# Fourier mixing with a soft mixture of experts, one core: two copies, one product and one pair of products moved in the written order

## The chip, the cores and the metric

The kernel runs on 1 core of one Trainium2 chip. The metric is the device time in microseconds of one execution. Engines are named as in the profile: PE (TensorE, matmuls; PEld its weight loads), DVE (VectorE), ACT (ScalarE), POOL (GpSimd) and SP (SyncE, whose queue issues most of the DMAs).

## The reference

```
X  = rfft(x, axis=1)                       # x: 8 batches, 2496 positions, 256 channels
Yr = Xr @ w_r - Xi @ w_i + b_r;  Yi = Xr @ w_i + Xi @ w_r + b_i
Y  = soft threshold of Yr and of Yi at 0.01
y  = irfft(Y)                              # the tokens, 8 * 2496 of them
logits = y @ phi                           # 32 slots = 8 experts x 4
d = softmax of logits over all tokens;  slot_input = d.T @ y
slot_out[e] = relu(slot_input[e] @ w1[e]) @ w2[e]
out = (softmax of logits over the slots) @ slot_out
```

All is float32. The softmax over tokens runs over all batches, so a running maximum and running sums go from batch to batch; the expert layers and the output come after the last batch.

## The kernel before, in words

The transform of length 2496 is split into 39 times 64. The work of one batch goes through stages, and at any moment three batches are in the kernel, each in another stage.

*First transform (`a_group`, L475 to L504).* From batch 2 on, a batch has 22 columns in six groups q: five of four columns and a last half group of two. POOL makes sums and differences of input rows (xh, xl), PE forms two products pa into two PSUM buffers, the first always in a buffer with the tag pf, the second with the tag that `PLAN["aqt"]` names: for the fifth group (q = 4) that is ps, for the half group pt. ACT copies the two products to the tile ast, at the times `PLAN["aqo"]` behind the group's own time: 0.4 and 0.7. A full ast tile is stored to DRAM by SP (`a_store`).

*Second transform and linear layer (`f2`, `lin_k`, `lin_y`, `tp_p`).* A batch has five steps s of four units of time each, so a batch has 20 units. In each step the stored data (ap) comes back, PE forms px twice, ACT and DVE split it into high and low parts (xsm and xth by ACT, then xsm and xtl by DVE, then xsh by ACT and xsl by POOL), PE forms pk and two products py, DVE adds them to ut, and the threshold gives rt. `tp_p` then multiplies with phi (pq), ACT copies the result to lg, and PE transposes it.

*Slot stage (`c_stages`, L795).* It runs for batches 0 to 6 beside later batches' transforms, with its time counted from t0 = 20 b + 26. `halves` (L752) does each of its four matrix products in two halves: for each half ACT makes a high part (the tiles chpg, chpL, chpe, chpd), DVE or POOL a low part (clpg and so on), and later PE does three matmuls into a PSUM buffer and an engine evacuates it. The four are pg (to g_sb, then through DRAM as gd and gp), pL (to L, the logits), pe (to ea, then through DRAM as ed and eb) and pd (to dd). Between pL and pe lie the maximum over tokens (DVE's mx, PE's pm, DVE's mall and dg, PE's pb) and the exponential ee. `running` (L899) forms the factor fo of the running maximum: two operations on DVE, then an exp on ACT at 12.2 + 0.4 units. pg and pe use the tag ps, which has a single buffer; so do pm and pb; pL uses ps and pt.

*Order.* No engine chooses: every engine and SP's queue run their instructions in program order. Program order comes from a heap of generators, each of which yields the time at which its next piece is written (`step_to`, `run_until`). The times stand in `PLAN`, some with other values for the last batches under `"late"`. They are units of that order only, and about 2.5 us of the trace go to one unit in the middle of the kernel.

```
"pL": [7.05, 8.02],          # the two halves' matmuls, behind t0
"pe": [12.02, 12.98],
"cl": [0.9, 0.4, 0.3],       # high part 0.9 ahead of the first matmul, second half 0.4 later, low part 0.3 later
```

In `halves` the evacuation of a half is written 0.25 behind its matmuls. `f2` writes the second px of a step at 4 (s - 1) + 2 units and its first two copies 0.59 later; `lin_y` writes the first half of a step's second py at 4 s + 2.35.

*After the last batch* the expert weights (loaded beforehand) are used in `mlp1` and `mlp2`, and the output is formed in blocks (pq, ost) and written by 41 DMAs.

Of the kernel before, what the change touches and what calls it, by code (L numbers as in the profile page):

```python
# [79 lines left out]
def _constants():  # L80
# [83 lines left out]

PLAN = {
    "aq": [-9.55, -5.55, -1.55, 2.45, 6.45, 7.4],
    "aqo": [0.4, 0.7],
    "aqt": ["pt", "pt", "pr", "pr", "ps", "pt"],
    "eo": {0: [5.0, 3.0], 4: [5.0, 4.95], 5: [2.05, 2.0]},
    "xq": [8.55] * 5 + [7.5],  # L170
    "aq2": {(2, 0): [6.6, 8.8, 9.2, 10.45], (2, 1): [8.8, 11.2, 11.6, 14.45]},
    "th": 'PA',
    "sh": 'A',
# [3 lines left out]
    "pL": [7.05, 8.02],  # L177
    "pm": 9.05,
    "pb": 10.32,
    "pe": [12.02, 12.98],  # L180
    "cm": 14.3,
    "pd": [19.05, 20.02],
    "pr": [20.48, 20.49, 24.48, 24.49, 28.49],
# [7 lines left out]
    "ko": 0.915,  # L191
    "to": 0.4,
    "ws": [-29, -28.9, -28.8, 2],
    "late": {'6': {'cms': [13.1, 13.2, 18, 22.65, 22.66, 22.67], 'pd': [16.681, 16.6], 'pdt': ('pl', 'pl'), 'pda': 1, 'pLt': ('ps', 'ps'), 'pr': [17.15, 18.3, 20.179, 19.707, 19.902], 'pL': [6.6, 7.3], 'pm': 8.51, 'pmr': 9.35, 'pb': 10.36, 'pe': [11.747, 11.96, 12.419], 'pg': [0.875, 1.275], 'fr': {'sinv': 0, 'm2': 0, 'f1': 0, 'suni': 0}, 'pbx': 1.2, 'pet': ('pf', 'pf'), 'so': 0.2}, '5': {'so': 1.5}, '4': {}},
    "T_": {'wl': [[-31, 't', 1], [-30, 't', 1], [-29, 't', 1], [-21.8, 't', 1], [-20.6, 't', 1], [-16.9, 't', 2], [-16.8, 't', 2], [-16.6, 't', 2], [-16.1, 't', 2], [-15.6, 't', 2], [-14.8, 'z', 2], [-14.6, 'z', 2], [-14.1, 'z', 2], [-13.6, 'Y', 1], [-13.1, 'Y', 1], [-12.4, 'c', 2], [-11.8, 's', 1], [-11.2, 'a', 1], [-10.6, 'a', 1], [-10, 'a', 1], [-9.5, 'Ww_r', 1], [-8.7, 'Wnws', 1], [-8.6, 'Wwd', 1], [0.01, 'k', 1], [0.01, 'u', 1], [0.02, 'x', 2], [0.02, 'x', 2], [0.02, 'x', 2], [1.4, 'R', 2], [1.4, 'R', 2], [1.73, 'Z', 2], [1.74, 'Z', 2]], 'cl': 2.0, 'cp': 46.5, 'ct': 46.6, 'du': [[2.55, 2]], 'd1': [], 'cm': [19.9, 19.91, 19.92, 25, 25.1, 25.2], 'cm7': [0.71, 1.7, 1.95, 2.7, 2.71, 2.8], 'ye': 0.2, 'te': [[5.6, 0.2], [5.5, 0.4]], 'pg': [-15.49, -11.49, -7.99, -3.934, -2.9], 'yt': 0.578, 'wr': -30.6, 'tp': [0, 0.6, 0.85, 0.5], 'tt': [0.4, 0.55, 0.821, 1.25, 0.994], 'z': 1.686, 'th': [0.1, 0.12], 'tl': [0.24, 0.25], 'pgt': ['ps', 'ps', 'ps', 'pf', 'pf'], 'ch': [0.263, 0.5, 0.7, 1.0, 1.514, 2.0], 'te7': 'AAAAAAAAAA', 'op': 2, 'ot': [3, 5, 7], 'gt': [-14.5, -10.5, -7.0, -3.93, -2.89]},
    "f1": [-1.6, -1.5],
    "kw": [[-28.6, 4], [-28.4, 12]],
# [62 lines left out]
def fourier_soft_moe_kernel(ctx: ExitStack, tc: tile.TileContext, t: dict, out: bass.AP):  # L260
# [18 lines left out]
    def psum(tag, name):  # L279
        return pp.tile([128, 512], F32, tag=tag, name=name, bufs=psum_bufs[tag])  # L280

    def wtile(shape, dt, tag, name):
        if tag in a_bufs:
            return wap.tile(list(shape), dt, tag=tag, name=name, bufs=a_bufs[tag])
        if tag in main_bufs:
            return wmp.tile(list(shape), dt, tag=tag, name=name, bufs=main_bufs[tag])
        return wcp.tile(list(shape), dt, tag=tag, name=name, bufs=chain_bufs[tag])
# [44 lines left out]
    def mm(**kw):  # L332
        tc.keep_in_program_order(nc.tensor.matmul(**kw))  # L333
# [11 lines left out]
    def load_x(i, q=sp):  # L345
        if i >= len(xorder) or xorder[i] in xrs:
            return
        b, g = xorder[i]
        ng = min(xc, G - g)
        xr = wtile([PX, xc, D], F32, "xr", f"xr{b}_{g}")  # L350
        q(out=xr[:, :ng, :], in_=x[b, :, g : g + ng, :])
        xrs[(b, g)] = xr
# [45 lines left out]
    ident, sgn, suni, sinv, dsc, dmask = (cols[k] for k in ("ident", "sgn", "suni", "sinv", "dsc", "dmask"))  # L398
    f1, m2 = cols["f1"][:P1], cols["m2"][:Q1]
# [75 lines left out]
    def a_group(b, q):  # L475
        n = GP if q < 5 else 1
        tx, te, to, tu = PLAN["aq2"].get((b, q), [20 * (b - 1) + PLAN["aq"][q] - d for d in (PLAN["xq"][q], *PLAN["eo"].get(q, PLAN["eo"][0]), 0)])
        yield tx
        load_x(xorder.index((b, 4 * q)))
        if q == 0:  # L480
            ad[b] = dr.tile([128 + 1, G, D], F32, tag="adr", name=f"adr{b}", bufs=3)
        xv = xrs[(b, 4 * q)].rearrange("p (g a) d -> p g a d", a=2)[:, :n]
        eo = []
        for i, z in enumerate(("xh", "xl")):
            yield (te, to)[i]
            eo.append(wtile([128, GP, D], F32, z, f"{z}{b}_{q}")[:, :n])
            P.tensor_tensor(out=eo[i], in0=xv[:, :, 0], in1=xv[:, :, 1], op=(ALU.add, ALU.subtract)[i])
        yield tu
        po = [psum(("pf", PLAN["aqt"][q])[i], f"pa{b}_{q}_{i}") for i in range(2)]
        for i in range(2):  # L490
            for c in range(2):
                rows = slice(64 * i, 64 * i + 64)
                mm(out=po[i][64 * c : 64 * c + 64, : n * D], lhsT=f1t[rows, 64 * c : 64 * c + 64], rhs=eo[c][rows],
                   start=True, stop=True, skip_group_check=True)
        for i in range(2):
            yield tu + PLAN["aqo"][i]
            g = 4 * q + n * i
            gs = next(a for a in abounds_[2] if a[0] <= g < a[1])
            if g == gs[0]:
                asts[(b, g)] = wtile([QA, 6, D], F32, "ast", f"ast{b}_{g}")  # L500
            ast = asts[(b, gs[0])]
            A.copy(out=ast[:, g - gs[0] : g - gs[0] + n, :].rearrange("p g d -> p (g d)"), in_=po[i][:, : n * D])
            if g + n == gs[1]:
                step_to(a_store(tu + PLAN["aqo"][i] + (1.35 if q == 5 else 0.75), b, ast, gs))  # L504

    def a_store(t0, b, ast, gs):
        yield t0
        a_write(ad[b], ast, *gs)
# [4 lines left out]
    def a_write(adr, ast, g0, g1, r0=0, r1=QA, q=sp):  # L513
        q(out=adr[r0:r1, g0:g1], in_=ast[r0:r1, : g1 - g0, :])
# [236 lines left out]

    def halves(n, t0, times, out, const, fr, src, evac, tags=("ps", "ps"), ev=0.25):  # L752
        xs = []
        for h in range(2 * fr[n]):
            yield t0 + (PLAN["chp"][h] if n == "suni" else times[0] - PLAN["cl"][0] + PLAN["cl"][1] * h)
            x = src(h)
            m, w = x.shape[0], x.shape[1] * x.shape[2]
            xh, xl = (
                wtile([128, 352], F32R, z, f"{z}{out[0]}_{h}")[:m, :w].rearrange("p (k s) -> p k s", s=S)
                for z in ("ch", "cl")  # L760
            )
            A.copy(out=xh, in_=x)
            yield t0 + (PLAN["clp"][h] if n == "suni" else times[0] - PLAN["cl"][0] + PLAN["cl"][1] * h + PLAN["cl"][2])
            {"V": V, "P": P}[PLAN["cl_"][n][h]].tensor_tensor(out=xl, in0=x, in1=xh.bitcast(F32), op=ALU.subtract)
            xs.append((xh, xl))
        for h in range(2):
            yield t0 + times[h]
            ps = psum(tags[h], f"{out[0]}_{h}")
            if fr[n]:
                ch, cl = const_hl[n]  # L770
                for i, (w_, x_) in enumerate(((ch, xs[h][0]), (cl, xs[h][0]), (ch, xs[h][1]))):
                    mm(out=out[1](ps), lhsT=w_, rhs=x_, start=i == 0, stop=i == 2)
            else:
                mm(out=out[1](ps), lhsT=const, rhs=src(h), start=True, stop=True)
            yield t0 + times[h] + ev
            evac(h, out[1](ps))
# [18 lines left out]
    def c_stages(b):  # L795
# [5 lines left out]
        g_sb = wtile([128, K1, S], F32, "g_sb", f"g_sb{b}")  # L801
        fr = K_["fr"]
        yield from halves(
            "sinv", t0, K_["pg"], (f"pg{b}", lambda ps: ps[:, :320]), sinv, fr,
            lambda h: p_sb[:, h * 10 : h * 10 + 10, :],
# [9 lines left out]
        yield t0 + K_["pL"][0] - PLAN["cl"][0] - 0.01  # L815
        gp_wrap(gp)
        yield from halves(
            "m2", t0, K_["pL"], (f"pL{b}", lambda ps: ps[:, :352]), m2, fr,
            lambda h: gp[:, h * 11 : h * 11 + 11, :],
# [167 lines left out]
    def step_to(gen):  # L987
        t = next(gen, None)
        if t is not None:
            heapq.heappush(heap, (t, next(seq), gen))  # L990
# [200 lines left out]
    for b in range(2, B):  # L1191
        for q in range(6):
            step_to(a_group(b, q))
# [231 lines left out]
    so = [wtile([128, D], F32R, "gp", f"so{i}") for i in range(2)]  # L1425
# [101 lines left out]
```

## Time and profile before

| | |
|---|---|
| median of 3 runs (504.04 to 506.6) | 504.19 us |
| the profiled execution | 506.02 us |
| its span, first to last instruction | 504.2 us |
| mean granted TensorE clock | 0.984 |
| PE busy | 479.7 us, 95% |
| DVE busy | 360.4 us, 71% |
| ACT busy | 315.9 us, 63% |
| POOL busy | 266.3 us, 53% |

A busy share says which engine is short of time, not what one place costs. For that one looks at the places where PE's row of matmuls has a hole, and at what the profile names as the releaser. In a timeline a line has the start, the duration, the engine, the operation and, in brackets, the idle time in front of it with the releaser; matmuls overlap, so their durations are longer than the distances between their starts.

### The profile page before, as it was taken

How to read it: one execution, taken by the hardware profiler on the slowest of the kernel's cores; microseconds unless marked ns; L12 is line 12 of the kernel's file. 1: busy time of each engine (PE TensorE's matmuls, PEld its weight loads, DVE VectorE, ACT ScalarE, POOL GpSimd, SP SyncE). 2: the span in 40 equal slices, each digit the busy share in tenths (PEclk: the TensorE clock that was granted, in tenths of full speed). 3: DMA queues.
4: the chain of work that ended last, by engine and by line, in shares of the span. 5: the costliest groups of instructions: out<-in, count | busy, mean ns of one | idle time of the engine just before them, and what ended most of it. 6: DMA issues, size and time to landing. Idle time of an engine off the chain costs nothing.

```text
span 504.2 us, 11938 instructions
## 1 busy us (share of the span) xinstructions
PE 479.7 (95%) x4438; PEld 392.4 (78%) x4438; DVE 360.4 (71%) x718; ACT 315.9 (63%) x724; POOL 266.3 (53%) x277
## 2 busy tenths in 40 slices
PE   8879999999999999999999999999999999999990
PEld 5479879788878877888788888879898777468880
DVE  3245996787878877987698769877976585446771
ACT  4357557667757775677577767775656556147770
POOL 0035777766956695769666966682344412322210
PEclk9988999999999999999999999999999999999996
DMA  8988698477969596959596969584878799449998
GB/s 294 319 288 303 237 281 257 140 249 231 289 185 301 156 299 200 296 151 326 144 309 161 320 189 318 112 307 119 240 174 246 294 400 387 171 162 401 404 405 332
DMA packets 90461, 131.04 MB, mean 260 GB/s; under 512 B 40204, under 2 KB 61836, under 8 KB 90404
## 3 DMA queue, kind: packets, MB, share of 16 engines
q1 hardware_dynamic: 89460, 128.16, 77.8%
q10 hardware_dynamic: 944, 2.13, 1.2%
q8 instruction: 35, 0.57, 0.5%
q14 instruction: 22, 0.18, 0.1%
HBM read 69.25 MB, written 50.00 MB: 237 GB/s over the span
## 4 chain that ended last, share of the span: by engine, by line
PE 70%; DVE 10%; DMA 10%; ACT 5%; issue 2%; SPq 1%; POOL 1%; ACTq 0%; DVEq 0%; POOLq 0%
PE py L333 16%; PE pq L333 10%; PE px L333 10%; PE pa L333 9%; PE pk L333 7%; PE pt L708 3%; PE pr L333 2%; DMA gd<-g_sb 2%; DMA gp<-gd 2%; PE pc L708 2%; PE pg L333 2%; DMA xr<-in_x 2%; DVE ut L256 2%; PE pe L333 1%; PE hps L333 1%
## 5 line engine op out<-in xcount | busy, mean ns | idle before, releaser
L256 POOL TENSOR_TENSOR xsl<-xsm,xsh 128x256 fp32r<-128x256 f32 x77 | 64.8, 843 | 112.1 <-ACT xsh L256 108.5
L256 DVE SCALAR_TENSOR_TENSOR ut<-py,pk,k 128x256 f32<-128x256 f32 x160 | 69.7, 477 | 29.0 <-PE py L333 27.7
L333 PE MATMUL px<-smov,ap 128*128 128x128 f32 x640 | 85.1, 277 | 1.3 <-ACT ast L256 1.3
L333 PEld LDWEIGHTS px<-smov,ap 128*128 128x128 f32 x640 | 79.5, 194 | 2.5 <-ACT ast L256 1.7
L256 ACT COPY ast<-pa 128x512 f32<-128x512 f32 (+1 forms) x88 | 48.1, 556 | 23.2 <-PE pa L333 23.1
L256 DVE TENSOR_TENSOR xtl<-px,xth 128x512 fp32r<-128x512 f32 x80 | 54.3, 680 | 0.1
L256 ACT CAST xth<-px 128x512 fp32r<-128x512 f32 x80 | 47.4, 594 | 6.8 <-PE py L333 5.9
L333 PE MATMUL py<-xth,nwsh 128*128 128x256 f32 (+1 forms) x160 | 51.4, 321 | 0.0
L256 DVE TENSOR_TENSOR xsm<-px,xsm 128x256 f32<-128x256 f32 x80 | 33.1, 414 | 25.5 <-ACT xth L256 14.0
L256 POOL TENSOR_TENSOR rt<-ut,rt 128x512 f32<-128x512 f32 x36 | 50.2, 1395 | 0.1
L333 PE MATMUL pk<-xsh,w_rh 128*128 128x256 f32 (+1 forms) x160 | 47.8, 299 | 0.0
L256 ACT COPY xsm<-px 128x256 f32<-128x256 f32 x80 | 29.9, 373 | 28.3 <-PE px L333 27.5
L256 POOL TENSOR_TENSOR xh<-xr 128x512 f32<-128x512 f32 (+1 forms) x36 | 44.7, 1241 | 1.0 <-DMA xr<-in_x 0.9
L333 PE MATMUL pk<-xsl,w_rh 128*128 128x256 f32 (+1 forms) x160 | 44.9, 281 | 0.3 <-POOL xsl L256 0.3
L333 PE MATMUL py<-xth,wdh 128*128 128x256 f32 (+1 forms) x160 | 45.1, 282 | 0.0
L333 PE MATMUL py<-xtl,nwsh 128*128 128x256 f32 (+1 forms) x160 | 44.9, 280 | 0.0
L333 PE MATMUL py<-xth,nwsl 128*128 128x256 f32 (+1 forms) x160 | 44.8, 280 | 0.0
L333 PE MATMUL py<-xtl,wdh 128*128 128x256 f32 (+1 forms) x160 | 44.8, 280 | 0.0
L333 PE MATMUL pk<-xsh,w_rl 128*128 128x256 f32 (+1 forms) x160 | 44.7, 279 | 0.0
L333 PE MATMUL py<-xth,wdl 128*128 128x256 f32 (+1 forms) x160 | 44.7, 279 | 0.0
L256 POOL TENSOR_TENSOR xl<-xr 128x512 f32<-128x512 f32 (+1 forms) x36 | 43.3, 1204 | 0.0
L256 ACT CAST xsh<-xsm 128x256 fp32r<-128x256 f32 x80 | 33.0, 412 | 16.4 <-DVE xsm L256 16.4
(227 smaller groups left out, 1274.7 us busy)
## 6 DMA issues: line engine op xcount, KB each, us to landing
ap<-adr SPq DMA_DIRECT2D x76, 256.0 KB
out<-ost SPq DMA_DIRECT2D x37, 512.0 KB
xr<-in_x SPq DMA_DIRECT2D x35, 512.0 KB
adr<-ast SPq DMA_DIRECT2D x20, 768.0 KB
y<-z SPq DMA_DIRECT2D x112, 96.0 KB
w<-in_moe_w SPq DMA_DIRECT2D x21, 512.0 KB
adr<-ast SPq DMA_DIRECT2D x7, 512.0 KB
w<-in_moe_w SPq DMA_DIRECT2D x14, 256.0 KB
```

The lines of the kernel that those rows point to most:

```text
L256: return lambda *a, **k: self.tc.keep_in_program_order(f(*a, **k))
L333: tc.keep_in_program_order(nc.tensor.matmul(**kw))
L708: tc.keep_in_program_order(nc.tensor.transpose(out=out, in_=in_, identity=identity))
```

## The change

Three edits of the written order; no instruction is added or taken away.

1. The second ast copy of the fifth and of the half group of `a_group` is written 0.5 behind the group's time in place of 0.7 (the third entry of `aqo`, picked by `2 * i`). For the fifth group this is between lg (at 0.45 on this scale) and xsh. The store of the half group's tile hangs on the same time and moves by 0.2 as well.
2. The first half of pe is written at 12.36 in place of 12.02, behind the first half of the second py (12.35). Its high and low parts keep their times: `first` in `halves` takes 12.02 for f1 from the new entry `clb`. The evacuation moves along, from 12.27 to 12.61.
3. In batch 5 the second half of pL is written at 7.95 in place of 8.02, so ahead of the px at 8.0.

```diff
-    "aqo": [0.4, 0.7],
+    "aqo": [0.4, 0.7, 0.5],
...
-    "pe": [12.02, 12.98],
+    "pe": [12.36, 12.98],
+    "clb": {"f1": 12.02},
...
-    "late": {... '5': {'so': 1.5}, '4': {}},
+    "late": {... '5': {'so': 1.5, 'pL': [7.05, 7.95]}, '4': {}},
...
         for i in range(2):
-            yield tu + PLAN["aqo"][i]
+            yield tu + PLAN["aqo"][i if q < 4 else 2 * i]
...
             if g + n == gs[1]:
-                step_to(a_store(tu + PLAN["aqo"][i] + (1.35 if q == 5 else 0.75), b, ast, gs))
+                step_to(a_store(tu + PLAN["aqo"][i if q < 4 else 2 * i] + (1.35 if q == 5 else 0.75), b, ast, gs))
...
         xs = []
+        first = PLAN["clb"].get(n, times[0])
         for h in range(2 * fr[n]):
-            yield t0 + (PLAN["chp"][h] if n == "suni" else times[0] - PLAN["cl"][0] + PLAN["cl"][1] * h)
+            yield t0 + (PLAN["chp"][h] if n == "suni" else first - PLAN["cl"][0] + PLAN["cl"][1] * h)
...
-            yield t0 + (PLAN["clp"][h] if n == "suni" else times[0] - PLAN["cl"][0] + PLAN["cl"][1] * h + PLAN["cl"][2])
+            yield t0 + (PLAN["clp"][h] if n == "suni" else first - PLAN["cl"][0] + PLAN["cl"][1] * h + PLAN["cl"][2])
```

## Rows read from the trace of the kernel before

**Rows 1.** Busy time by stretch: start:end, sum, then each engine, clock, DMA share, GB/s.
```profile
180.00:230.00 50.00, 49.49 (x491) 41.64 (x491) 40.65 (x81) 34.74 (x81) 35.51 (x36) 1.00 0.79 243
...
460.00:470.00 10.00, 10.00 (x56) 8.28 (x55) 6.92 (x11) 7.77 (x18) 3.70 (x4) 1.00 1.02 406
```

**Rows 2.** Waits of PE and its weight loads, 88 to 368 us: total, times, longest.
```profile
PE pg L333 <- ACT ast L256: 2.5, 6, 0.5
PE pb L333 <- DVE dg L256: 0.6, 1, 0.6
...
PEld pe L333 <- DVE clpe L256: 2.1, 6, 0.4
```

**Rows 3.** Timeline of PE around the first pg, batches 0 and 2: start, duration, instruction.
```profile
92.98 0.42 PE L333 MATMUL pg<-chpg,sinvh 128*128 128x320 f32 x1 [0.51 <-ACT ast L256]
...
93.63 0.43 PE L333 MATMUL pa<-xl,f1t 64*64 64x256 f32 x1
...
189.78 0.28 PE L333 MATMUL py<-xth,wdl 128*128 128x256 f32 x1
189.90 0.28 PE L333 MATMUL py<-xtl,wdh 128*128 128x256 f32 x1
190.62 0.41 PE L333 MATMUL pg<-chpg,sinvh 128*128 128x320 f32 x1 [0.44 <-ACT ast L256]
...
191.26 0.43 PE L333 MATMUL pa<-xh,f1t 64*64 64x256 f32 x1
```

**Rows 4.** Timeline of ACT at the same place, batches 0 and 2.
```profile
92.02 0.42 ACT L256 CAST xsh<-xsm 128x256 fp32r<-128x256 f32 x1
...
188.41 0.27 ACT L256 COPY lg<-pq 128x128 f32<-128x128 f32 x1
189.68 0.41 ACT L256 CAST xsh<-xsm 128x256 fp32r<-128x256 f32 x1 [1.00 <-DVE xsm L256]
189.99 0.58 ACT L256 COPY ast<-pa 128x512 f32<-128x512 f32 x1
```

**Rows 5.** Timelines of DVE and POOL at the same place, batches 0 and 2.
```profile
92.94 0.73 POOL L256 TENSOR_TENSOR xsl<-xsm,xsh 128x256 fp32r<-128x256 f32 x1
...
189.56 0.68 DVE L256 TENSOR_TENSOR xtl<-px,xth 128x512 fp32r<-128x512 f32 x1
...
190.17 1.07 POOL L256 TENSOR_TENSOR xsl<-xsm,xsh 128x256 fp32r<-128x256 f32 x1 [1.20 <-ACT xsh L256]
```

**Rows 6.** Timeline of PE, batch 2: both pe and the py behind each.
```profile
215.74 0.41 PE L333 MATMUL pe<-chpe,f1h 117*120 117x352 f32 x1
...
216.62 0.29 PE L333 MATMUL py<-xth,nwsh 128*128 128x256 f32 x1
...
219.42 0.41 PE L333 MATMUL pe<-chpe,f1h 117*120 117x352 f32 x1
...
219.99 0.28 PE L333 MATMUL py<-xth,nwsh 128*128 128x256 f32 x1
```

**Rows 7.** Timeline of DVE, batch 2: the first low part for pe.
```profile
215.53 0.77 DVE L256 TENSOR_TENSOR clpe<-ee,chpe 117x352 fp32r<-117x352 f32 x1 [0.49 <-ACT chpe L256]
```

**Rows 8.** Timelines of ACT (batches 2 and 5) and PE (batch 5) between the two pe.
```profile
218.54 0.20 ACT L256 ACTIVATE fo<-fo 128x1 f32<-128x1 f32 x1 [0.51 <-DVE fo L256]
...
365.48 0.20 ACT L256 ACTIVATE fo<-fo 128x1 f32<-128x1 f32 x1 [0.20 <-DVE fo L256]
...
365.65 0.40 PE L333 MATMUL pe<-chpe,f1h 117*120 117x352 f32 x1
...
366.73 0.46 ACT L256 COPY ea<-pe 120x352 f32<-120x352 f32 x1
```

**Rows 9.** Chain that ended last, batch 5: start, length, what.
```profile
367.20 5.07 DMA ed<-ea
```

**Rows 10.** Timelines of ACT and DVE, batch 5, ahead of the maximum mx.
```profile
354.32 0.45 ACT L256 COPY L<-pL 128x352 f32<-128x352 f32 x1 [0.26 <-PE pL L333]
...
354.67 0.70 DVE L256 STREAM_TRANSPOSE z<-rt 128x512 f32<-128x512 f32 x1
```

More of the change, by code (lines that the diff above doesn't have):

```diff
@@ L193 @@
     "ws": [-29, -28.9, -28.8, 2],
-    "late": {'6': {'cms': [13.1, 13.2, 18, 22.65, 22.66, 22.67], 'pd': [16.681, 16.6], 'pdt': ('pl', 'pl'), 'pda': 1, 'pLt': ('ps', 'ps'), 'pr': [17.15, 18.3, 20.179, 19.707, 19.902], 'pL': [6.6, 7.3], 'pm': 8.51, 'pmr': 9.35, 'pb': 10.36, 'pe': [11.747, 11.96, 12.419], 'pg': [0.875, 1.275], 'fr': {'sinv': 0, 'm2': 0, 'f1': 0, 'suni': 0}, 'pbx': 1.2, 'pet': ('pf', 'pf'), 'so': 0.2}, '5': {'so': 1.5}, '4': {}},
+    "late": {'6': {'cms': [13.1, 13.2, 18, 22.65, 22.66, 22.67], 'pd': [16.681, 16.6], 'pdt': ('pl', 'pl'), 'pda': 1, 'pLt': ('ps', 'ps'), 'pr': [17.15, 18.3, 20.179, 19.707, 19.902], 'pL': [6.6, 7.3], 'pm': 8.51, 'pmr': 9.35, 'pb': 10.36, 'pe': [11.747, 11.96, 12.419], 'pg': [0.875, 1.275], 'fr': {'sinv': 0, 'm2': 0, 'f1': 0, 'suni': 0}, 'pbx': 1.2, 'pet': ('pf', 'pf'), 'so': 0.2}, '5': {'so': 1.5, 'pL': [7.05, 7.95]}, '4': {}},
     "T_": {'wl': [[-31, 't', 1], [-30, 't', 1], [-29, 't', 1], [-21.8, 't', 1], [-20.6, 't', 1], [-16.9, 't', 2], [-16.8, 't', 2], [-16.6, 't', 2], [-16.1, 't', 2], [-15.6, 't', 2], [-14.8, 'z', 2], [-14.6, 'z', 2], [-14.1, 'z', 2], [-13.6, 'Y', 1], [-13.1, 'Y', 1], [-12.4, 'c', 2], [-11.8, 's', 1], [-11.2, 'a', 1], [-10.6, 'a', 1], [-10, 'a', 1], [-9.5, 'Ww_r', 1], [-8.7, 'Wnws', 1], [-8.6, 'Wwd', 1], [0.01, 'k', 1], [0.01, 'u', 1], [0.02, 'x', 2], [0.02, 'x', 2], [0.02, 'x', 2], [1.4, 'R', 2], [1.4, 'R', 2], [1.73, 'Z', 2], [1.74, 'Z', 2]], 'cl': 2.0, 'cp': 46.5, 'ct': 46.6, 'du': [[2.55, 2]], 'd1': [], 'cm': [19.9, 19.91, 19.92, 25, 25.1, 25.2], 'cm7': [0.71, 1.7, 1.95, 2.7, 2.71, 2.8], 'ye': 0.2, 'te': [[5.6, 0.2], [5.5, 0.4]], 'pg': [-15.49, -11.49, -7.99, -3.934, -2.9], 'yt': 0.578, 'wr': -30.6, 'tp': [0, 0.6, 0.85, 0.5], 'tt': [0.4, 0.55, 0.821, 1.25, 0.994], 'z': 1.686, 'th': [0.1, 0.12], 'tl': [0.24, 0.25], 'pgt': ['ps', 'ps', 'ps', 'pf', 'pf'], 'ch': [0.263, 0.5, 0.7, 1.0, 1.514, 2.0], 'te7': 'AAAAAAAAAA', 'op': 2, 'ot': [3, 5, 7], 'gt': [-14.5, -10.5, -7.0, -3.93, -2.89]},
```

## The prediction

> **What bounds the kernel now.** The page comes first: PE is busy for 95% of the span. By stretches it is more one-sided still: in 50 us of the middle PE is busy for 49.49, at a granted clock of 1.00, while DVE has 40.65, ACT 34.74 and POOL 35.51 [rows 1]. The six middle batches are thus a row of matmuls with hardly a hole, and the end comes earlier only by what is cut out of PE's row. Behind it the output is written at 406 GB/s with a DMA share of 1.02 (second line of [rows 1]); its length is fixed, but it begins with the first output block, so a lead that PE has by then reaches the end whole.
>
> So the view to read next is PE's waits. From 88 to 368 us PE waits for ACT's ast at pg (six times, 2.5 us) and for DVE's dg at pb (0.6 us); its weight loads add pe waiting for DVE's clpe (six times, 2.1 us) [rows 2]. The three edits touch these places. Their prices I take from start to start of matmuls, since busy spans of matmuls overlap and hide part of a hole.
>
> **First edit: the second ast copy behind lg.** In batch 2 the last py matmul starts 0.12 after its neighbour, at 189.90; pg starts at 190.62, 0.72 later [rows 3]. The hole is 0.60. Read the same way it is 0.67 in batch 0, 0.60, 0.60, 0.61, 0.59 in batches 1 to 4 and 0.42 in batch 5, 3.5 us in all. pg and the fifth group's second product share the one ps buffer, so pg waits for the ast copy that empties it. ACT issues that copy behind xsh: lg is done at 188.68, xsh starts only at 189.68, after an idle 1.00 for DVE's xsm, and ast at 189.99 [rows 4]. Directly behind lg it runs from about 188.6 to 189.2, inside ACT's idle time, and delays xsh by nothing. pg then follows py at 190.02. Its own operand clpg doesn't become the next wait: it stands on DVE two places ahead of xtl, which starts at 189.56 [rows 5]. So in batches 1 to 5 the whole hole goes: 2.82 us. In batch 0 ACT has no idle time there; copy and xsh change places, the copy starts at 92.02 [rows 4] in place of 0.31 later, and pg moves from 92.98 to 92.68, 0.3 of its 0.67. Sum 3.12 us. xsh is then 0.5 late in batch 0, but xsl, which reads it, starts at 92.94 [rows 5], behind other POOL work, anyway.
>
> What is late next? The half group's pa goes into the pf buffer that xtl empties. In batch 2 xtl ends at 190.24 [rows 5]; pa would start at 190.66 in place of 191.26 [rows 3]. The cover is 0.42 us, and about the same in batches 1, 3, 4 and 5. The half group's own second copy runs right behind its first already, so 0.2 units earlier are worth nothing there; its store passes one y transfer on SP's queue, which puts that y transfer one issue later, long before its reader, and frees SP a little sooner for the next ap loads. Taken as zero. Bounds of this edit: a gain of 3.5 us (all holes) and of 0.3 us (if pa is held, below).
>
> [...]
>
> **Second edit: the first pe behind py.** Before, the first pe takes from 215.74 to the start of py at 216.62; the second, with ready operands, from 219.42 to 219.99 [rows 6]. 0.88 against 0.57: 0.31 us per batch is lost, because the third matmul needs clpe, which DVE ends at 216.30 [rows 7]. Over six batches that is 1.9 us. With six py matmuls ahead (0.12 each and a restart, 0.8 us), pe starts at 216.5 and its third matmul at 216.9, 0.6 after clpe. The stall goes; the ACT and DVE work that makes chpe and clpe keeps its place, since the diff holds its times at 12.02.
>
> The price is on ACT. The evacuation ea moves from 12.27 to 12.61 units, behind xsm and xth (12.59) and also behind the exp of fo (12.60), which waits for DVE's queue. In batch 2 fo starts at 218.54, after 0.51 of waiting for DVE [rows 8]. ea follows at about 218.65 and ends at 219.10. The second pe needs the same single ps buffer; PE now comes to it at 219.42 - 0.31 = 219.11, and with the 0.05 that pg needs behind the end of ast [rows 3, 4] it starts at 219.15: 0.04 lost. Batches 1, 3 and 4 give the same sum. ast, lg and T, queued behind ea on ACT, move by up to 0.35 us; idle time in front of T and of the next xsm takes that up. So batch 0, which has no fo, brings 0.31, and batches 1 to 4 bring 0.27 each: 1.39 us.
>
> Batch 5 is the exception. No pa stands between its two pe, so PE would be at the second at 365.65 - 0.31 = 365.34, but fo starts at 365.48 [rows 8]; ea runs from 365.58 to 366.03 and the second pe starts at 366.08, 0.43 later than before. The second ea, at 366.73 before, then starts at 366.88. Behind it lies a chain that PE does wait for: ed with 5.07 us of transfer [rows 9], eb, dd and pz. PE's own 0.43 is absorbed in its waits there, and ea's 0.15 is passed on. Net of the second edit: 1.39 - 0.15 = 1.24 us gain. Bounds: a gain of 1.9 us, and a loss of 1.8 us if the second pe came 0.43 late in each of batches 1 to 5 (0.31 - 5 x 0.43). I stay near the upper one, since four batches of six have batch 2's rows.
>
> [...]
>
> **Third edit: batch 5's two pL together.** The second pL moves ahead of px; PE's row holds the same matmuls. The second L copy, at 354.32, could start about 0.35 earlier. But the maximum mx that reads L stands on DVE behind the transpose z, which runs from 354.67 to 355.37, and L was complete at 354.77 [rows 10]. So mx, and with it pb, stays where it is, and px is 0.5 later with nobody waiting. Value zero; bounds 0.8 us gain (pb's wait of 0.6 gone with its restart) and 0.5 us loss (px's delay in full).
>
> **Sum.** 3.12 + 1.24 + 0 = 4.36 us. The profiled execution's span of 504.2 becomes 499.8; with what lies around the span its 506.02 becomes 501.7. It was 1.8 us above the median of the runs, 504.19; the same 4.36 off the median gives the prediction, **499.8 us**. All bounds together would reach from 498.0 (6.2 gained) to 506.2 (2.0 lost).
>
> **Rivals.**
> *pa is held by POOL (0.13).* In batch 2 pa starts at 191.26, right as xsl ends at 191.24 [rows 3, 5], and four more batches look alike; xsl hangs on xsh, which the edit doesn't move. If that is a true wait, pg's lead is lost at pa: the first edit brings only batch 0's 0.3, in all 1.5 us: 502.7. Against it: in batch 0 pa starts at 93.63 while xsl runs on to 93.67.
> *Third edit works (0.10).* If mx can start earlier after all, pb no longer waits: 499.8 - 0.8 = 499.0. Against it, z.
> *Half is given back (0.09).* The cover of 0.42 us at pf is short; if each batch gives back half of its gain at such a place, 502.0.
> *Slower (0.06).* fo becomes the gate of the second pe in every batch from 1 to 5. The place is ea behind fo on ACT; it decides from the point where fo is ready 0.9 us later against PE than read now (5 x 0.87 eats the 4.36). At 1.2 us later, batches 1 to 4 lose 0.93 each and batch 5 1.35, 5.1 in all; less 3.12 and batch 0's 0.31 that makes 505.8. For it: fo already waits for DVE. Against it: DVE's order ahead of fo is unchanged.
>
> **Chances.** The forecast has 0.62. What a measurement can tell from no change is about 0.5%, 2.5 us, so the border is 501.7. Faster: 0.62 + 0.10 = 0.72. Same: 0.13 + 0.09 = 0.22. Slower: 0.06. The range runs from 498.4 (the third edit works and the second loses nothing at fo) to 502.3 (a little over half given back).
>
> **What would show it.** First edit right: ast directly behind lg on ACT, no PE wait for ast at pg in batches 1 to 5, a short one in batch 0. Wrong: a new wait at the half group's pa or the px after it. Second: the first pe's three matmuls evenly spaced behind py, the second pe without a hole above 0.1 in batches 1 to 4, and a wait of some 0.7 us for ea in batch 5. Third: mx still right behind z, pb still waiting. The whole is wrong if a middle batch doesn't get shorter by 0.8 to 0.9 us.

## The result: 498.16 us, and the profile after

The changed kernel took 498.16 us (median of 4 runs, 496.96 to 499.96); the kernel before took 505.13 beside it (4 runs, 504.04 to 506.60). The ratio is 0.9863, 95% interval 0.9820 to 0.9907, so 4.7 to 9.1 us faster. A second comparison later gave 498.91 (6 runs) against 504.61 (23 runs), 0.9881 (0.9850 to 0.9912). The ratios here and below leave out runs in a slower state, so they differ a little from the quotient of the medians. The forecast was 499.8, its range 498.4 to 502.3: the direction is right, the size too small.

| | before | after |
|---|---|---|
| the profiled execution | 506.02 us | 496.96 us |
| its span | 504.2 us | 495.1 us |
| mean granted TensorE clock | 0.984 | 0.992 |
| PE busy | 479.7 us, 95% | 473.5 us, 96% |
| DVE busy | 360.4 us, 71% | 355.9 us, 72% |
| ACT busy | 315.9 us, 63% | 316.4 us, 64% |
| POOL busy | 266.3 us, 53% | 269.1 us, 54% |

Stretches that answer to [rows 1], in the same columns:

```profile
175.00:225.00 50.00, 49.97 (x500) 42.49 (x499) 40.44 (x82) 35.77 (x85) 36.62 (x36) 1.00 0.82 251
451.00:461.00 10.00, 10.00 (x56) 8.30 (x55) 6.96 (x12) 7.77 (x18) 3.71 (x4) 1.00 1.02 405
```

The middle had 0.51 us of idle PE in 50; it has 0.03. The output stretch is as before, at 405 GB/s. The waits between 85 and 361 us, which answer to [rows 2]:

```profile
PE pb L334 <- DVE dg L257: 0.7, 2, 0.5
PEld pe L334 <- ACT ea L257: 0.7, 1, 0.7
...
PE pe L334 <- ACT ea L257: 0.5, 1, 0.5
...
PE pg L334 <- ACT ast L257: 0.2, 1, 0.2
```

pg waits for ast once (batch 0) instead of six times, the waits for clpe are gone, and one wait is new: a pe for ea, in batch 5. At pg, in batches 0 and 2, for [rows 3]:

```profile
89.47 0.41 PE L334 MATMUL pg<-chpg,sinvh 128*128 128x320 f32 x1 [0.21 <-ACT ast L257]
89.72 0.31 PE L334 MATMUL pg<-chpg,sinvl 128*128 128x320 f32 x1
...
185.05 0.28 PE L334 MATMUL py<-xtl,wdh 128*128 128x256 f32 x1
185.17 0.31 PE L334 MATMUL pg<-chpg,sinvh 128*128 128x320 f32 x1
185.31 0.31 PE L334 MATMUL pg<-chpg,sinvl 128*128 128x320 f32 x1
185.46 0.31 PE L334 MATMUL pg<-clpg,sinvh 128*128 128x320 f32 x1
185.70 0.43 PE L334 MATMUL pa<-xh,f1t 64*64 64x256 f32 x1
```

In batch 2 pg follows py by 0.12. Compare also the next distance, to pg's second matmul: 0.14 here, and 0.25 in batch 0, where pg still waits. In the kernel before it was 0.25 in batch 2 as well:

```profile
190.62 0.41 PE L333 MATMUL pg<-chpg,sinvh 128*128 128x320 f32 x1 [0.44 <-ACT ast L256]
190.87 0.31 PE L333 MATMUL pg<-chpg,sinvl 128*128 128x320 f32 x1
```

So the pg matmul behind a hole costs about 0.10 more to its successor. ACT at the same place, for [rows 4], and POOL, for [rows 5]:

```profile
183.56 0.27 ACT L257 COPY lg<-pq 128x128 f32<-128x128 f32 x1
183.73 0.59 ACT L257 COPY ast<-pa 128x512 f32<-128x512 f32 x1
184.84 0.41 ACT L257 CAST xsh<-xsm 128x256 fp32r<-128x256 f32 x1 [0.52 <-DVE xsm L257]
```

```profile
185.33 1.06 POOL L257 TENSOR_TENSOR xsl<-xsm,xsh 128x256 fp32r<-128x256 f32 x1 [1.20 <-ACT xsh L257]
```

pa starts at 185.70 while xsl runs on to 186.39: POOL does not hold it. At the two pe, batches 2 and 5, for [rows 6, 8]; first PE, then ACT:

```profile
210.97 0.33 PE L334 MATMUL pe<-chpe,f1h 117*120 117x352 f32 x1
211.13 0.32 PE L334 MATMUL pe<-chpe,f1l 117*120 117x352 f32 x1
211.29 0.32 PE L334 MATMUL pe<-clpe,f1h 117*120 117x352 f32 x1
...
357.31 0.42 PE L334 MATMUL pe<-chpe,f1h 117*120 117x352 f32 x1 [0.48 <-ACT ea L257]
```

```profile
356.71 0.20 ACT L257 ACTIVATE fo<-fo 128x1 f32<-128x1 f32 x1 [1.02 <-DVE fo L257]
356.82 0.43 ACT L257 COPY ea<-pe 120x352 f32<-120x352 f32 x1
```

The first pe's matmuls are 0.16 apart, the stall for clpe is gone. In batch 5 ea stands behind fo, and PE waits. Ahead of the maximum mx of batch 5, for [rows 10], ACT and DVE:

```profile
344.78 0.86 ACT L257 COPY L<-pL 128x352 f32<-128x352 f32 x2
```

```profile
345.94 0.70 DVE L257 STREAM_TRANSPOSE z<-rt 128x512 f32<-128x512 f32 x1
346.56 1.35 DVE L257 TENSOR_REDUCE mx<-L 117x32 f32<-117x704 f32 x1
```

L was complete at 345.64; mx still starts only as z ends, at 346.56.

How the two first traces differ, by the starts of the same matmul (after minus before, change from one landmark to the next; my working from the timelines):

| | forecast | these two traces | five more traces with edits 1 and 2 |
|---|---|---|---|
| up to the first transform's pa at 56 us | 0 | -3.20 | |
| pg, batch 0 | -0.30 | -0.31 | -0.30 to -0.31 |
| pg, batches 1 to 4, each | -0.60 | -0.59 to -0.62 | -0.59 to -0.62 |
| pg, batch 5 | -0.42 | -0.41 | -0.40 to -0.42 |
| second half of pg, batches 1 to 5, each | 0 | -0.10 to -0.12 | -0.09 to -0.12 |
| second pe, batches 0 to 4, each | -0.31, then -0.27 | -0.27 to -0.29 | -0.27 to -0.32, once -0.40 |
| second pe, batch 5 | +0.43 | +0.42 | +0.42 and +0.43 (fo where it was) |
| all from pL of batch 5 to pm of batch 6, the line above in it | +0.15 | -0.79 | |

In the first column of traces the rows of edit 1 make 3.1 us and, with the second half of pg, 3.7; edit 2 up to batch 4 makes 1.4. That is 5.1 us, and it repeats in every trace with the two edits. The remaining 4.0 of the 9.1 us between the two spans are the head (the stretch up to 56 us, whose code is the same in both) and the end of the slot stage, and the experiments are about these.

### The profile page after: what moved, and what is told of

Read it like the earlier page. It is cut to its first block, busy times and chain, and to the rows that moved or that the text cites. A ratio compares the mean times of both kernels' runs of the same rounds, so it can differ in the third digit from the quotient of the medians.

```text
span 495.1 us, 11946 instructions
## 1 busy us (share of the span) xinstructions
PE 473.5 (96%) x4438; PEld 388.8 (79%) x4438; DVE 355.9 (72%) x718; ACT 316.4 (64%) x724; POOL 269.1 (54%) x277
## 4 chain that ended last, share of the span: by engine, by line
PE 77%; DMA 9%; DVE 6%; ACT 2%; SPq 2%; issue 1%; POOL 0%; ACTq 0%; DVEq 0%
PE py L334 19%; PE px L334 11%; PE pq L334 11%; PE pk L334 9%; PE pa L334 8%; PE pt L709 4%; PE pr L334 3%; DMA w<-in_moe_w 3%; DMA gd<-g_sb 2%; PE pc L709 2%; SPq L328 2%; DMA xr<-in_x 2%; PE pg L334 1%; PE pe L334 1%; PE hps L334 1%; PE po L334 1%
## 5 line engine op out<-in xcount | busy, mean ns | idle before, releaser
L257 POOL TENSOR_TENSOR xl<-xr 128x512 f32<-128x512 f32 (+1 forms) x36 | 46.3, 1286 | 0.0
L334 PE MATMUL pq<-rhs,ct 128*128 128x512 f32 x156 | 41.7, 405 | 0.2
```

Of the source, the lines that this page charges most:

```text
L257: return lambda *a, **k: self.tc.keep_in_program_order(f(*a, **k))
```

## The experiments

**Each edit alone, and the first two together.** Four kernels beside each other; the kernel before took 504.52 (23 runs).

```diff
# edit 1 alone, in the kernel before
-    "aqo": [0.4, 0.7],
+    "aqo": [0.4, 0.7, 0.5],
-            yield tu + PLAN["aqo"][i]
+            yield tu + PLAN["aqo"][i if q < 4 else 2 * i]
...
# edit 2 alone: the changed kernel with this and edit 3 undone
-    "aqo": [0.4, 0.7, 0.5],
+    "aqo": [0.4, 0.7, 0.7],
# edits 1 and 2 together: the changed kernel with only this undone
-    '5': {'so': 1.5, 'pL': [7.05, 7.95]}
+    '5': {'so': 1.5}
# edit 3 alone: that entry in the kernel before
```

> Only the first edit: the second ast copy of the fifth and the half group behind lg; pe and pL as before. Theory: pg's hole goes (3.2 us) and with it the restart that a matmul behind a hole pays, 0.10 in each of batches 1 to 5 (pg's second matmul 0.25 behind its first before, 0.15 after), in all 3.7 us faster than before. Rival, my prediction's sum: 3.1 us, no restart in it. Rival, the edits work only together: under 2 us. In the profile both theories want pg's three matmuls 0.15 apart in batches 1 to 5 or not.

Measured: 499.16 (6 runs), ratio 0.9876 (0.9831 to 0.9921).

> Only the second edit: the first pe behind py, ea behind fo. Theory: 1.4 us in batches 0 to 4; in batch 5 the second pe 0.43 us late and passed on as 0.15, so 1.2 us faster. Rival: the chain from ea through ed, eb and dd gets shorter by the edit, as the profile after shows (0.7 us between the second pe and pz in batch 5): then 1.9 us or more, and the profile of this kernel shows the same shortening.

Measured: 503.19 (12 runs), ratio 0.9959 (0.9929 to 0.9990).

> Only the third edit: batch 5's second pL ahead of px. Theory: 0 us, mx starts behind z as before and pm and pb wait as before (from py to pm 0.5 us). Rival: the third edit is what brought pm and pb 0.5 us forward after the change: 0.5 to 0.8 us faster, and the distance from py to pm falls to 0.15.

Measured: 504.84 (12 runs), ratio 1.0002 (0.9966 to 1.0037).

> The first and second edit together, the third undone. Theory: as fast as the whole change within 0.3 us, and 4.9 us faster than before, with pm and pb of batch 5 where the arrival of gp puts them in this execution. Rival (third edit counts): 0.5 to 0.8 us slower than the whole change.

Measured: 499.48 (6 runs), ratio 0.9864 (0.9817 to 0.9911).

So nothing of the third edit can be told from noise (1.7 us faster to 1.9 slower), and the 0.13 by which pm of batch 5 comes earlier in its trace is gp's, which landed 0.13 sooner; the first two together are as fast as the whole change within the noise. Each trace has the steps of its own edits as in the table: edit 1 is worth 3.7 and edit 2 1.4 where they act. But the median of edit 1 alone lies 5.4 us below before, with an interval of 4.0 to 8.5. In its trace there is something else, at pL of batch 6, and it works against it:

```profile
390.31 1.09 PE L333 MATMUL pL<-gp,pk 120*128 120x352 f32 x2 [2.31 <-DMA gp<-gd]
390.71 0.90 PE L333 MATMUL py<-xth,nwsh 128*128 128x256 f32 x1
391.41 0.41 PE L333 MATMUL py<-xth,nwsl 128*128 128x256 f32 x1
391.63 0.41 PE L333 MATMUL py<-xtl,nwsh 128*128 128x256 f32 x1
```

PE waited 2.31 us for gp, and then its matmuls stand 0.21 apart instead of 0.12. By windows of 2 us (columns as in [rows 1]):

```profile
388.00:390.00 2.00, 0.00 (x1) 0.00 (x0) 0.00 (x0) 0.00 (x0) 0.00 (x0) 1.00 0.85 286
390.00:392.00 2.00, 1.69 (x6) 1.36 (x7) 0.83 (x2) 1.91 (x6) 0.00 (x0) 0.69 1.04 350
392.00:394.00 2.00, 2.00 (x11) 2.00 (x10) 0.79 (x2) 0.83 (x3) 0.73 (x1) 0.50 1.00 375
```

Behind these 2.31 us of idle PE the granted clock is 0.69 from 390 to 392 us and 0.50 from 392 to 394. In the traces whose clock stayed at 1.00, pm of batch 6 starts 6.40 behind this pL; here, with the lower clock, it is 7.96. So this stretch took 1.6 us more in this execution, on top of a wait of 2.3. The first trace of before has the like in its head: PE idle 2.02 at 33.85, for rows of the input that came late, and then a clock of 0.50 (34 to 40 us):

```profile
34.00:40.00 6.00, 5.26 (x18) 4.30 (x19) 3.91 (x9) 2.83 (x6) 3.82 (x4) 0.50 0.95 300
```

In all other traces of this study the head, the same code, is 1.1 to 3.9 us shorter.

**The store or the copy?** All traces with edit 1 have pm of batch 5 0.37 earlier; gp of batch 5 lands sooner there, and the half group's store stands at another place on SP's queue. The store and the fifth group's copy were each tried alone in the kernel before. Before took 504.61 (23 runs) in this comparison.

```diff
# the store alone
-                step_to(a_store(tu + PLAN["aqo"][i] + (1.35 if q == 5 else 0.75), b, ast, gs))
+                step_to(a_store(tu + PLAN["aqo"][i] + (1.15 if q == 5 else 0.75), b, ast, gs))
# the fifth group's copy alone ("aqo" with its third entry)
-            yield tu + PLAN["aqo"][i]
+            yield tu + PLAN["aqo"][2 * i if q == 4 else i]
```

> The kernel before with one thing moved: the store of the half group's ast tile is written 0.2 units earlier (1.15 instead of 1.35 behind the copy), the copies keep their places. In all kernels with the first edit, pm of batch 5 starts 0.36 to 0.37 earlier against its neighbours and pb another 0.12 to 0.16; there SP issues the store ahead of the first y transfer behind gp, in the others behind it, and gp is landed 3.4 to 3.65 us after its issue instead of 4.07 to 4.24. Theory A, the store's place makes gp land earlier: here too adr stands right behind gp on SP, ACT's copy of gp starts 3.4 to 3.7 us after gp's issue, pm of batch 5 comes 0.36 earlier and pb 0.1 to 0.2 more, everything else as before: 0.5 us faster than before. Rival B, the copies' place does it (ACT or PE at another phase): gp lands 4.1 us after its issue as before, pm and pb of batch 5 stay, 0.0 us.

Measured: 504.41 (12 runs), ratio 0.9984 (0.9953 to 1.0015). gp lands 3.69 after its issue, pm of batch 5 0.38 earlier.

> The kernel before with the first edit for the fifth group alone: its second copy directly behind lg; the half group's copies and its store keep their places. Theory A: pg starts 0.31 earlier in batch 0, 0.60 to 0.62 in batches 1 to 4, 0.42 in batch 5, and the second half of pg another 0.10 in batches 1 to 5 (the matmul behind a hole no longer takes 0.25 in place of 0.15 to its successor), 3.7 us in all, and pm and pb of batch 5 keep their places: 3.7 us faster than before, 500.8 where before has 504.5. Rival B, the whole of the first edit's gain comes from the copies: pm and pb of batch 5 move as well, 4.2 us. Rival C, the store was what gained most of the 5.4 us by which the medians with the first edit alone lay below before: here 2 us or less.

Measured: 502.89 (12 runs, 498.44 to 504.41), ratio 0.9950 (0.9923 to 0.9978). pg and its second half gain as in theory A. But pm of batch 5 moves too (0.37, gp in 3.70 us), though the store stands behind the y transfer as before. Neither theory A stands: each half of the edit seemed to bring the same gain. That called for more traces of before.

The times don't add up either. By time the copy alone brings 1.7 us (1.1 to 3.9), though its trace has all 3.7 us of steps, and the store alone 0.2 (2.4 faster to 0.8 slower); the whole first edit had brought 5.4 (4.0 to 8.5). Rival C, that the store is what gained most, fits the time of the copy alone and not that of the store alone. The runs of one kernel spread over 3 to 7 us here, and no trace shows a step that would make up the difference; it stays open.

**The kernel before, traced twice more.** No edit.

> The kernel before once more, for its trace alone. Open is how much of the difference between the two first traces (9.0 us at the end, while the medians differ by 7.0 and the steps that repeat add up to 5.2) belongs to single executions. Theory A, chance of the execution: the head is 2 to 3 us shorter than in the first trace (no fall of the granted clock at 34 us), gp of batch 5 may land in under 3.7 us here too and then pm of batch 5 comes 0.37 earlier. Theory B, the first edit's own: gp of batch 5 needs 3.9 to 4.3 us as in the three traces without that edit, where the seven with a part of it had 3.2 to 3.7.

> The same, a second time, with the same two theories. In both, pg, the first pe and the steps of batches 0 to 4 lie within 0.05 of the first trace.

Measured: 505.99 and 502.67. The heads are 2.6 and 3.0 us shorter than the first, at a granted clock of 1.00 from 30 to 90 us. In both gp of batch 5 lands in 3.8 us, and pm comes 0.34 and 0.37 earlier. So the 0.37 can come without any edit: the first trace of before had a late gp there, and I had compared with an unlucky execution. Whether the store makes the early gp surer is open: it landed in 3.2 to 3.7 us in all eight traces with the store moved, and in 3.7 to 4.2 us in the six without, and pm was late in three of those six. The steps of batches 0 to 4 lie within 0.12 of the first trace (forecast 0.05). What the first of the two had instead is a late gp of batch 6:

```profile
394.70 0.83 PE L333 MATMUL pL<-gp,pk 120*128 120x352 f32 x2 [2.05 <-DMA gp<-gd]
```

```profile
394.00:396.00 2.00, 1.30 (x7) 1.12 (x8) 0.44 (x2) 1.52 (x5) 0.00 (x0) 0.96 1.02 409
396.00:398.00 2.00, 2.00 (x10) 1.86 (x9) 1.31 (x3) 1.22 (x4) 0.70 (x1) 0.50 1.03 416
```

Again 2 us of idle PE (2.05) and then a clock of 0.50 (396 to 398 us), and again pm of batch 6 comes 1.6 late behind pL (7.95). In the second of the two the wait was 0.96 and the clock stayed at 1.00.

**The late pe of batch 5 taken away.** In the changed kernel fo is written behind the first ea. The changed kernel ran again beside it.

```diff
-        yield t0 + PLAN["mo"] + 0.4
+        yield t0 + PLAN["mo"] + 0.42
```

> The changed kernel with the exp of fo written 0.02 units later, so that ACT has the first ea ahead of fo in batches 1 to 5. Theory A, fo on ACT is what the second pe of batch 5 waits for (0.48 of idle PE and a restart): ea starts right behind xth, the second pe of batch 5 starts 0.6 to 0.7 earlier, behind pt, batches 1 to 4 keep their times within 0.05, and the end comes 0.4 to 0.7 earlier than in the changed kernel: 497.6 where that has 498.2. Rival B, the late pe is absorbed at PE's later waits for pd and pz of batch 5, as the prediction had it: the second pe is 0.6 earlier, but pd is not, and the time stays. Rival C, fo late holds acc on DVE and with it xsm: some batch gets longer by 0.1 to 0.5.

Measured: 498.75 (6 runs), ratio 0.9874 (0.9838 to 0.9910).

> The changed kernel again, for its level and its trace beside the three others. By the steps of aligned traces the change is worth 4.2 us (first edit) and 1.0 us (second edit: 0.28 in batches 0 to 4, less 0.42 in batch 5), 5.2 in all, so 499.3 where before has 504.5. If the measured 7.0 us of the first comparison are the change's own, 497.5.

Measured: 498.91 (6 runs), ratio 0.9881 (0.9850 to 0.9912). The two have the same span, 495.0, but the head with fo moved happened to be 0.7 shorter; behind the head its trace is 0.8 longer. In the trace with fo moved, ACT and PE of batch 5:

```profile
355.27 0.45 ACT L257 COPY ea<-pe 120x352 f32<-120x352 f32 x1
356.29 0.20 ACT L257 ACTIVATE fo<-fo 128x1 f32<-128x1 f32 x1 [0.57 <-DVE fo L257]
```

```profile
356.15 0.41 PE L334 MATMUL pe<-chpe,f1h 117*120 117x352 f32 x1
...
386.78 0.83 PE L334 MATMUL pL<-gp,pk 120*128 120x352 f32 x2 [0.92 <-DMA gp<-gd]
```

The second pe is 0.73 earlier against its neighbours, as theory A has it, and its lead lasts past pd and pz. Then pL of batch 6 waits 0.92 for gp, where the same kernel with the late pe waits 0.20 in one trace and not at all in the other. So rival B is right, but at another place than the prediction named. The transfers go with it. SP issues an ap load, two loads of expert weights and another ap load shortly ahead of gd of batch 6. Over the traces (times from the start of the second half of pg of batch 6; 11.05 from there to pL is PE's own work, the rest is waiting):

| trace | last ap issued | gd issue to gp issue | pL later than 11.05 |
|---|---|---|---|
| before, first trace (PE 0.9 late at pd and pz of batch 5) | -2.6 | 5.7 | 0.1 |
| before, the two later traces | -2.7, -1.9 | 7.9, 6.8 | 2.2, 1.1 |
| edit 1 alone, edit 3 alone | -2.1, -2.3 | 7.5, 7.6 | 2.5, 1.5 |
| store alone, copy alone | -2.6, -1.9 | 6.3, 7.4 | 1.0, 1.1 |
| changed kernel, fo moved | -2.3 | 6.2 | 1.1 |
| changed kernel twice, edits 1 and 2 | -2.8, -3.8, -3.4 | 5.2, 4.8, 5.7 | 0.4, 0.0, 0.4 |
| edit 2 alone | -2.8 | 5.2 | 0.1 |

In the five traces in which PE comes late to pg (four with the late pe, and the first of before, late at pd and pz), pL starts 0.0 to 0.4 late; in the seven others 1.0 to 2.5. So the late pe's 0.42 is paid at pe, and as much or more is saved at pL. That it is the lead of the loads on gd which does this is argued and not shown: all leads of 2.8 us or more go with 4.8 to 5.7 us from gd to gp, but at about the same lead (2.6 and 2.7) gd took 5.7 us in the first trace of before and 7.9 in the second.

**The loads out of the way.** Two weight loads go behind gp of batch 6, once with fo moved, once in the changed kernel. Before took 504.81 (9 runs).

```diff
-    "T_": {'wl': [..., [-21.8, 't', 1], [-20.6, 't', 1], ...
+    "T_": {'wl': [..., [-16.97, 't', 1], [-16.95, 't', 1], ...
```

> The changed kernel with two moves: the exp of fo behind the first ea, and the two loads of expert weights that SP issues ahead of gd of batch 6 put behind gp of batch 6. With fo alone moved, the second pe of batch 5 started 0.73 earlier than in the changed kernel and the span stayed at 495.0, because pL of batch 6 then waited 0.92 for gp. Theory A: gd stands behind those loads in the DMA engines (share 0.91 to 1.18 from 370 to 380 us, gd landed 6.2 us after its issue), so an earlier PE only waits longer there. Without the loads gd lands in 3 to 4.5 us, pL of batch 6 has no wait, and the 0.7 to 0.9 us reach the end: 497.3 to 497.8 where the changed kernel has 498.2 to 498.9; against the kernel before 0.986. Rival B: gd's and gp's landing have nothing to do with the loads, the wait stays at 0.9 and so does the time. Rival C: the loads come late for the expert layers, which then wait, and the time gets longer by up to the 2 x 1.3 us that they take at 400 GB/s.

Measured: 497.26 (5 runs), ratio 0.9852 (0.9832 to 0.9873).

> The changed kernel with only the two loads of expert weights put behind gp of batch 6. There pL of batch 6 waits 0.2 for gp or not at all. Theory A of the same call: 0.0 to 0.3 us faster than the changed kernel, since here PE has a 0.42 late second pe of batch 5 in the same place. Rival B: the same time. Rival C: up to 2.6 us slower, as in the other kernel of this call.

Measured: 497.72 (4 runs), ratio 0.9862 (0.9846 to 0.9878). pL waits in neither (11.05 and 11.06 from pg). gd still takes 5.2 us, not 3 to 4.5 as I expected, but 5.2 is soon enough. Neither trace separates the loads from a late PE, though. The changed kernel has its late pe, and waited little or not at all before. With fo moved PE lost its lead elsewhere in the profiled execution: eb landed a us later than in most traces, PE reached pz 1.3 us later against its second pe than in the trace with fo alone moved, and

```profile
370.16 0.41 PE L334 MATMUL pd<-clpd,sunih 128*128 128x320 f32 x1 [0.39 <-POOL clpd L257]
```

The medians lie 1.65 and 1.2 us under the changed kernel's 498.91 of the comparison before, with narrower spreads (496.0 to 499.2, 497.6 to 498.5, against 496.75 to 501.01), but the intervals overlap, and the first comparison gave the changed kernel 498.16: that either version beats it is not shown.

## Why the prediction was right in direction and too small

*First edit: right in mechanism, mis-sized.* "In batches 1 to 5 the whole hole goes: 2.82 us" and 0.3 in batch 0 came out as 2.8 and 0.31. The term that failed is what I took as the whole: the second half of pg comes another 0.10 to 0.12 earlier in five batches, 0.53 us. I priced a hole from the last py to the first pg and left out that pg's first matmul behind it is itself slower to its successor (0.25 against 0.14 in batch 2); at pb I did speak of a restart. 3.7 in place of 3.12. By my own test the whole was wrong if a middle batch didn't get shorter by 0.8 to 0.9 us; it got shorter by 1.0 (0.60, 0.11 and 0.28).

The idle column of the timelines prices this edit lower: PE's waits for ast at pg are 2.5 us before [rows 2] and 0.2 after, so by it the edit would have brought 2.3. The starts moved by 3.1, and by 3.7 with the second matmul: here the idle column shows only a part of what a hole took.

*Rivals.* POOL does not hold pa (pa at 185.70, xsl to 186.39), nothing is given back at pf, and fo gates the second pe in batch 5 only: in batches 1 to 4 the steps are 0.27 to 0.29 against 0.27 forecast. These three are refuted in every trace.

*Second edit: right up to batch 4 (1.4 us), wrong behind it.* The failed step is "PE's own 0.43 is absorbed in its waits there, and ea's 0.15 is passed on. Net of the second edit: 1.39 - 0.15". The second pe of batch 5 came 0.42 late, as forecast to 0.01. But at pd and pz PE waited only in two traces, in which eb was late (the first of before, and the one with fo and the loads moved). In the traces with the late pe and nothing else late, the 0.42 runs on to pg of batch 6. I had priced what follows from one trace, in which eb was late and gp of batch 6 was not. In the usual execution it is gp of batch 6 that PE waits for, and there a later PE waits less. From pL of batch 5 to pm of batch 6 the changed kernel (two traces) and edits 1 and 2 together take 49.2 to 49.8 us (mean 49.6); the six traces of kernels that lack one of the two edits, and in which the clock did not fall here, take 50.0 to 50.7 (mean 50.3). The stage is thus 0.7 shorter on average, where I had forecast 0.15 longer. With the two traces in which the wait was longest and the clock fell, the mean is 50.9 and the stage 1.4 shorter. How much of this is the late pe, and how much the draw of a few executions, is not settled.

ACT ran ea and fo of batch 5 in the order in which they are written: ea ran behind fo, which had waited 1.02, and with the order swapped it ran 1.02 ahead of it.

*Third edit: right.* mx stands behind z as before, and alone the edit makes 1.0002 (0.9966 to 1.0037).

*The sum.* 5.1 us repeat in each trace, 0.7 more come on average at the end of the slot stage: 5.8, against 5.7 in the second comparison and 7.0 in the first. From the median that I started from, 504.19, this would give 498.4, the low end of my range. The rest of the first comparison, 1.2 us, is inside its interval; 0.7 of it is there if the two traces with the fall of the clock at pL are counted, and the rest I do not explain: before's median was 504.5 to 505.1 in the four comparisons. The range was built from the bounds of the three edits alone; the runs shown already spread over 2.5 us, and that spread belonged into it.

## What to carry to other kernels

The hole at pg cost its length from start to start plus a slower pair behind it (0.10 us), so price a hole up to the second matmul behind it. Before a stage's waits are priced, look whether they are the program's or one execution's: here the wait for a transfer with others queued ahead of it was 0, 0.96 and 2.05 us in three executions of one kernel. A lead that is won ahead of such a wait can be given back there, and a place that is late ahead of it may cost nothing. Where PE waits for a round trip through DRAM, look at what the queue issued just ahead of it before moving anything on PE: gd to gp took 4.8 to 7.9 us here. That it was the loads ahead of gd is not shown.

## What the runs showed of the hardware

- The granted clock fell to 0.50 after PE had been idle for 2.02, 2.05 and 2.31 us (the head of the first trace of before, and pL of batch 6 in its second trace and with edit 1 alone). From pL to pm the two executions in which it fell there took 7.95 and 7.96 us, those in which it stayed at 1.00 took 6.40: 1.6 us beyond the wait. It stayed at 1.00 there after waits of 0.88 to 1.30. The length of the idle time alone does not tell the two apart: in the third trace of before PE was idle for the same 2.02 ahead of a matmul on the input at 16.44, and the clock was 1.00 from 0 to 20 us and from 20 to 30.
- The first pg matmul (128x320, granted clock 1.00) takes 0.25 to its successor's start behind a wait of 0.21 and 0.14 without one, at the same place of the program.
- The same pair of transfers through DRAM (gd, then gp of batch 6, 320 KB and 320 KB by the issue list) took between 8.9 and 12.1 us from the first issue to ACT's first read, over the 14 traces; what decides it is not shown.
